# Transposes of the second read on VectorE, and a decode of the weights in three VectorE operations, in a fused attention and MLP kernel

## The chip, the cores and the metric

One Trainium2 chip, one of its cores. The metric is the device time of one execution in microseconds (us). The kernel before took a median of 690.48 us over three runs (689.43 to 690.51).

## The reference

```python
# x [8, 8, 512, 64], state [8, 8, 32, 64] (float32); B, H, S or Ns, D
a     = softmax(scale * x @ state^T, over the 32 states);  xread = a @ state
a2    = softmax(scale * state @ x^T, over the 512 tokens); sread = a2 @ x
attn  = concatenate([xread, sread], axis=2)        # [8, 8, 544, 64]
rows  = attn.transpose(0, 2, 1, 3).reshape(8 * 544, 512)
out   = (maximum(rows @ w_in, 0) ** 2) @ w_out     # w_in [512, 2048], w_out [2048, 512]
```

The weights come as 64-bit floats, so each is two 32-bit words, a low and a high one.

## The kernel before

The work is cut into blocks. Blocks 0 to 7 are the 512 token rows of one batch each; block 8 is the 256 rows of all `sread`. In a block, the hidden layer is cut into 16 chunks of 128 columns (`fc`). For each chunk, `hidden` multiplies on TensorE into a tile `ph` (L688 or, through the helper `mm3`, L306), ScalarE and VectorE make relu and square of it (L697 to L715), and `accumulate` multiplies the result with 128 rows of `w_out` into four accumulators `acc` (L306 or L722). TensorE's order is the next chunk's `hidden`, then this chunk's `accumulate`.

For blocks 0 to 7 the attention is folded into the weights: `make_w2` multiplies the batch's state with `w_in` (tile `w2ps`), 256 or 512 columns at a time, and `hidden` multiplies that `w2` with the softmax `k` of the batch, so `xread` itself is never made. Most operands are split into a high and a low part, and three matmuls (high by high, high by low, low by high) stand for one; that is `mm3`. In block 0, the first eight chunks of `hidden` (`plain_w2`, L688) and the first six of `accumulate` (`plain_wo`, L722) use the f32 values unsplit. `prep_wo` decodes a chunk of `w_out`, `split_wo` splits it.

The attention of a batch runs one block ahead of its use. For a batch from 2 on: `load_p` and `load_n` load x in two layouts, `xp` (in runs of 128 bytes) and `xn`; `prep` transposes `xp` on VectorE into `xT`; `scores` (tile `sc`) multiplies the states with it; `transposed_scores` and `softmax` make `k` on VectorE and ScalarE; `exp_s` (L500) makes the exponentials `e` of the second softmax; `transposes` (L566) turns `e` on TensorE into a tile `pt`, which is copied to `eT`; `sread` (L587) multiplies `eT` with `xn` into `pr`, whose scaled and transposed result goes to the SBUF tile `srall`. `move_sread` collects `srall` for block 8. Batch 0 has a way of its own: `prep` transposes on TensorE (tile `px`), `token_scores` gives `tsc`, and `token_softmax` ends in transposes into `pk` and a copy to `kf`. The tiles `sc`, `w2ps`, `pt`, `pr` and `tsc` share one pair of PSUM banks (`banks`); the tiles `ph` take turns in two others.

`decode` makes an f32 from the two words of a 64-bit float: ScalarE takes the absolute value of the high word (L321); VectorE clamps it (L323), shifts it by three bits and masks (L325), puts sign and top bit in (L327), and the low word's top three bits (L330). `decode_wi` does so for `w_in` (16 tiles `wi_raw`), `prep_wo` for `w_out` (16 tiles `wo_raw`). The result is kept in f32.

The order of everything is written by hand in the strings `FIRST` (blocks 0 to 2 and what goes with them), `BLOCK` (one later block, filled in for blocks 3 to 6), `LAST` and `READS`. A word names a step; a word with a tilde runs the step to its next `yield`, one without runs it to its end. `keep_order` ties each engine's instructions to that order, so every engine's queue, and SyncE's queue of transfers, is in the order of the words. The string `SECOND` lists the steps that take the second of two ways.

Of the kernel before, what the change touches and what calls it, by code (L numbers as in the profile page):

```python
# [14 lines left out]
ALU = mybir.AluOpType
# [25 lines left out]
    token_softmax.0.1 load_wo.5 prep_wo.0 ~hidden.0.0 ~prep_wo.1 ~prep_wo.1 ~prep_wo.1 ~w2.0.1
    hidden.0.0 prep_wo.1 ~hidden.0.1 ~decode_wi.4 ~decode_wi.5 w2.0.1 ~decode_wi.4 ~decode_wi.5 load_wo.6
    ~decode_wi.4 scores.0
    hidden.0.1 ~decode_wi.5 decode_wi.4 accumulate.0.0 ~exp_s.0.0 decode_wi.5 ~exp_s.0.0 ~prep_wo.2 exp_s.0.0
    ~exp_s.0.1 load_wo.7 ~decode_wi.6 ~prep_wo.2 ~exp_s.0.1 ~hidden.0.2 ~prep_wo.2 ~split_wo.0 exp_s.0.1 prep_wo.2
    ~decode_wi.7 ~transposes.0 split_wo.0
    hidden.0.2 ~decode_wi.6 accumulate.0.1 ~decode_wi.7 transposes.0 ~decode_wi.6 ~decode_wi.7 ~decode_wi.6
    ~prep_wo.3 ~decode_wi.7 ~prep_wo.3 ~prep_wo.3 ~prep_wo.3 ~w2.0.2 ~split_wo.1 prep_wo.3 ~hidden.0.3 w2.0.2
    decode_wi.6 decode_wi.7 ~sread.0 split_wo.1
    hidden.0.3 prep_states.1 accumulate.0.2 load_states.2 ~sread.0 ~prep_wo.4 sread.0 start.2 ~prep_wo.4 ~prep_wo.4  # L50
    ~prep_wo.4 ~prep_wo.6 prep_wo.4 ~prep.1.0 ~split_wo.2 ~prep_wo.6 ~prep_wo.6 ~hidden.0.4 split_wo.2 prep.1.0
    ~prep_wo.6 ~prep_wo.5 prep.1.1 prep_wo.6 ~prep.1.2
# [874 lines left out]
```

## Time and profile before

| | |
|---|---|
| median of the runs | 690.48 us |
| the profiled execution | 689.09 us |
| its span, first to last instruction | 687.3 us |
| busy: TensorE, its weight loads, VectorE, ScalarE | 96%, 72%, 53%, 50% |
| busy from 0 to 30 us: TensorE, VectorE, ScalarE | 17.0, 19.1, 13.3 us |
| first `hidden` starts | 27.58 us |
| moved by DMA | 48.47 MB, 79,845 packets |

The profile is one execution on the chip. Times in its rows are in us unless marked ns; L306 is line 306 of the kernel. PE is TensorE, PEld its weight loads (which overlap the matmuls), DVE VectorE, ACT ScalarE, SP SyncE, which issues most transfers. A row of the timeline gives start, length, engine, line, operation, tiles (written, then read) with their shape, and in brackets how long the engine had been idle and who ended that. The chain of waits follows the work that ended last back from its end. A matmul in f32 shows as two records; a transpose shows as one.

### The profile page before, as it was taken

What the parts mean: (1) busy time and instruction counts of PE and PEld (TensorE: products, weight loads), DVE (VectorE), ACT (ScalarE), POOL (GpSimd) and SP (SyncE); (2) the same over time, 40 slices, a digit from 0 to 9 for tenths busy, and PEclk for the clock granted to TensorE, in tenths of its full rate; (3) what the DMA queues carried; (4) which work ended last, traced back from release to release, by engine and by line L of the source; (5) the groups of instructions that cost most, each with busy time, mean ns of one, the idle gap of its engine ahead of it and who ended that gap; (6) DMA issues with size and microseconds to landing.
All of it is one profiled execution on the core that took longest, in us unless ns stands there. A gap on an engine that the chain in (4) does not pass through costs nothing.

```text
span 687.3 us, 9880 instructions
## 1 busy us (share of the span) xinstructions
PE 660.9 (96%) x3904; PEld 497.7 (72%) x3904; DVE 365.7 (53%) x668; ACT 340.8 (50%) x627; POOL 1.2 (0%) x7
## 2 busy tenths in 40 slices
PE   4799999999999999999999999999999999999994
PEld 3444667777777777678777777777767877778993
DVE  4888976889343634554446434552455332235541
ACT  4466656767555544454436434453445444444441
POOL 0000000000000000000000000000000000000000
PEclk9999999999999999999999999999999999999998
DMA  9904351738030553302040024002100011001001
GB/s 319 320 13 112 110 166 33 256 111 185 0 123 1 143 103 80 55 1 55 22 108 1 1 62 116 7 1 62 62 0 1 1 45 48 0 1 50 13 1 31
DMA packets 79845, 48.47 MB, mean 71 GB/s; under 512 B 57912, under 2 KB 66616, under 8 KB 79800
## 3 DMA queue, kind: packets, MB, share of 16 engines
q1 hardware_dynamic: 79256, 47.33, 24.8%
q8 instruction: 30, 0.49, 0.3%
q10 hardware_dynamic: 544, 0.52, 0.3%
q14 instruction: 15, 0.12, 0.1%
HBM read 35.26 MB, written 12.06 MB: 69 GB/s over the span
## 4 chain that ended last, share of the span: by engine, by line
PE 92%; ACT 3%; DVE 2%; DMA 0%; issue 0%; SPq 0%; DVEq 0%; ACTq 0%
PE acc L306 50%; PE ph L306 28%; PE w2ps L311 5%; PE acc L722 3%; PE ph L688 2%; PE pr L587 1%; PE sc L311 1%; PE pt L566 1%; ACT e L500 1%; PE tsc L446 1%; ACT ph L707 0%; ACT ph L708 0%; ACT g_hi L713 0%; DMA std<-in_state_dram 0%; DVE dec L327 0%
## 5 line engine op out<-in xcount | busy, mean ns | idle before, releaser
L306 PE MATMUL acc<-wo,g_hi 128*128 128x512 f32 x1040 | 322.7, 391 | 0.4 <-DVE o L739 0.4
L306 PEld LDWEIGHTS acc<-wo,g_hi 128*128 128x128 f32 x1040 | 193.1, 188 | 43.2 <-issue 2.5
L306 PE MATMUL acc<-wo,g_lo 128*128 128x512 f32 x520 | 202.5, 389 | 0.0
L715 DVE TENSOR_TENSOR g_lo<-ph,g_hi 128x512 fp32r<-128x512 f32 (+1 forms) x138 | 91.0, 659 | 195.3 <-ACT g_hi L713 191.9
L306 PE MATMUL ph<-k_hi,w 128*128 128x512 f32 x480 | 171.8, 399 | 0.0
L707 ACT ACTIVATE ph<-ph 128x512 f32<-128x512 f32 x92 | 53.6, 582 | 158.1 <-PE ph L306 158.1
L306 PEld LDWEIGHTS ph<-k_hi,w 128*128 128x128 f32 x480 | 90.0, 188 | 45.4 <-issue 27.7
L306 PEld LDWEIGHTS acc<-wo,g_lo 128*128 128x128 f32 x520 | 97.6, 188 | 21.1 <-DVE g_lo L715 0.2
L713 ACT CAST g_hi<-ph 128x512 fp32r<-128x512 f32 (+1 forms) x138 | 77.6, 563 | 34.7 <-DVE ph L712 31.8
L306 PE MATMUL ph<-k_lo,w 128*128 128x512 f32 x240 | 93.4, 389 | 0.0
L712 DVE SCALAR_TENSOR_TENSOR ph<-ph,r 128x512 f32<-128x512 f32 (+1 forms) x46 | 27.9, 606 | 63.1 <-ACT r L711 63.1
L711 ACT ACTIVATE r<-ph 128x512 f32<-128x512 f32 (+1 forms) x46 | 24.1, 525 | 71.8 <-PE ph L306 71.8
L708 ACT ACTIVATE ph<-ph 128x512 f32<-128x512 f32 x92 | 53.5, 582 | 2.9
L306 PEld LDWEIGHTS ph<-k_lo,w 128*128 128x128 f32 x240 | 45.1, 188 | 8.2
L645 DVE TENSOR_TENSOR w<-w2ps,w 128x512 fp32r<-128x512 f32 x60 | 38.6, 686 | 18.9 <-ACT w L642 18.9
L642 ACT CAST w<-w2ps 128x512 fp32r<-128x512 f32 x60 | 32.4, 595 | 13.9 <-PE w2ps L311 13.9
L311 PE MATMUL w2ps<-wi,stT 64*32 64x512 f32 (+1 forms) x544 | 35.8, 583 | 2.1 <-ACT e L500 2.1
L306 PE MATMUL ph<-sr_k_hi,s 128*128 128x256 f32 x128 | 25.5, 282 | 0.0
L722 PE MATMUL acc<-deco,gf 128*128 128x512 f32 x48 | 21.9, 599 | 0.0
L306 PEld LDWEIGHTS ph<-sr_k_hi,s 128*128 128x128 f32 x128 | 21.0, 191 | 0.7
L306 PE MATMUL ph<-sr_k_lo,s 128*128 128x256 f32 x64 | 18.1, 283 | 0.0
L311 PEld LDWEIGHTS w2ps<-wi,stT 64*32 64x32 f32 x544 | 6.2, 105 | 16.2 <-issue 10.4
(87 smaller groups left out, 460.2 us busy)
## 6 DMA issues: line engine op xcount, KB each, us to landing
out_dram<-o SPq DMA_DIRECT2D x34, 256.0 KB, 2.5
wi_raw<-in_moe_w_in_dram SPq DMA_DIRECT2D x16, 512.0 KB, 5.2
wo_raw<-in_moe_w_out_dram SPq DMA_DIRECT2D x16, 512.0 KB, 6.7
xp<-in_x_dram SPq DMA_DIRECT2D x96, 64.0 KB, 2.3
part_d<-po SPq DMA_DIRECT2D x8, 256.0 KB, 2.3
o<-part_d SPq DMA_DIRECT2D x8, 256.0 KB, 3.4
xn<-in_x_dram SPq DMA_DIRECT2D x6, 256.0 KB, 8.4
kl<-k_d SPq DMA_DIRECT2D x2, 512.0 KB, 4.0
```

What stands on the lines that cost most here:

```text
L306: T.matmul(ps, l, r, start=first and i == 0, stop=last and i == len(seq) - 1)
L311: T.matmul(ps, l, r, start=True, stop=True)
L642: A.copy(w[:, u, g, 0], ps[g])
L645: V.tensor_sub(w[:, u, g, 1], ps[g], w[:, u, g, 0].bitcast(F32))
L688: T.matmul(ph, w[c][:, cs], k[:, c], start=c == 0, stop=c == G - 1)
L707: A.activation(ph, ph, AF.Relu)
L708: A.activation(ph, ph, AF.Square)
L711: A.activation(r, ph, AF.Relu)
L712: V.scalar_tensor_tensor(ph, ph, 0.0, r, ALU.max, ALU.mult)
L713: A.copy(ghi, ph)
L715: V.tensor_sub(glo, ph, ghi.bitcast(F32))
L722: T.matmul(acc[i], ghi[:, ts(i, P)], wo[fc], start=first, stop=last)
```

## The change

- **Decode.** For all 32 tiles, ScalarE scales the absolute high word by 2 to the 16th, and a second ScalarE operation makes the three low bits from the top byte of the low word, into a new tile `bits` with one buffer. VectorE then clamps, shifts by three and ors the bits, and ors the sign: three operations in place of four.
- **Second read.** For batches 3 to 7 (`b >= ND`), `transposes` runs on VectorE in blocks of 32 by 32 into `eB`; four transfers write it to a tensor in DRAM, `e_d`, and one loads it back as `eT`. `pr` then takes a buffer of `ph` in place of the pair of banks.
- **Read results.** `sread` writes its result to a tensor in DRAM, `sr_d`, and `move_sread` loads it with four transfers in place of sixteen. The columns are ordered by state, then batch, and the last store follows.
- **Dummies.** `keep_busy` issues matmuls of the identity with itself ahead of the first steps of batch 0, into the tile that the step then writes; their number is in `BUSY`, 39 in all.
- **Table.** The first step runs an exponential of one column on ScalarE.
- **Chunk 6** of block 0's `accumulate` is unsplit (`plain_wo`).
- **Order.** At the start, x of batch 0 is loaded ahead of the weights, and the first token scores go ahead of most decodes. From then on `w2` stands later, and `transposes` earlier, than before.

TensorE at the start: `px` transposes of x, `tsc` token scores, `w2ps` the first w2 (before, then changed).

```order
L417 MATMUL px0_0_133<-ident_70,xn0_89 128x128 x4
L417 MATMUL px0_1_140<-ident_70,xn0_89 128x128 x4
L417 MATMUL px0_2_151<-ident_70,xn0_89 128x128 x4
L446 MATMUL tsc0_161<-bd_83,xT0_132 128x64 x8
L417 MATMUL px0_3_177<-ident_70,xn0_89 128x128 x4
L446 MATMUL tsc0_161<-bd_83,xT0_132 128x64 x8
L311 MATMUL w2ps0_0_1_217<-wi0_73,stT_72 32x256
```

In the changed kernel, on the same engine and at the same place:

```order
L319 MATMUL px0_1_141<-ident_70 128x128 x3
L446 MATMUL px0_1_141<-ident_70,xn0_94 128x128 x4
L319 MATMUL px0_2_154<-ident_70 128x128 x2
L446 MATMUL px0_2_154<-ident_70,xn0_94 128x128 x4
L319 MATMUL tsc0_166<-ident_70 128x128 x3
L476 MATMUL tsc0_166<-bd_88,xT0_129 128x64 x8
L319 MATMUL px0_3_188<-ident_70 128x128 x2
L446 MATMUL px0_3_188<-ident_70,xn0_94 128x128 x4
L319 MATMUL tsc0_166<-ident_70 128x128 x4
L476 MATMUL tsc0_166<-bd_88,xT0_129 128x64 x8
L319 MATMUL w2ps0_0_0_235<-ident_70 128x128 x8
L324 MATMUL w2ps0_0_1_236<-wi0_72,stT_71 32x256
```

The steps keep their order; dummies (L319) stand ahead of each, six more ahead of the first `px`.

VectorE at the start, from the last decode operations ahead of the first token softmax (`m10` its maximum, `sp0_0` the subtraction) on, before:

```order
L323 TENSOR_SCALAR dec3_159<-dec3_159 128x512
L325 TENSOR_SCALAR dec3_159<-dec3_159 128x512
L327 SCALAR_TENSOR_TENSOR dec3_159<-wi_raw3_109,dec3_159 128x512
L454 TENSOR_REDUCE m10_0_184<-tsc0_161 128x16
L458 TENSOR_TENSOR sp0_0_192<-tsc0_161,m10_0_184 128x512
L330 SCALAR_TENSOR_TENSOR wi0_73<-wi_raw2_105,dec2_149 128x2x256
```

In the changed kernel, from VectorE's first instruction on:

```order
L383 STREAM_TRANSPOSE stA0_111<-std0_89 128x256
L338 TENSOR_SCALAR dec0_152<-dec0_152 128x512
L340 SCALAR_TENSOR_TENSOR dec0_152<-dec0_152,bits0_164 128x512
L343 SCALAR_TENSOR_TENSOR wi0_72<-wi_raw0_107,dec0_152 128x2x256
L484 TENSOR_REDUCE m10_0_195<-tsc0_166 128x16
L488 TENSOR_TENSOR sp0_0_201<-tsc0_166,m10_0_195 128x512
L338 TENSOR_SCALAR dec1_181<-dec1_181 128x512
L340 SCALAR_TENSOR_TENSOR dec1_181<-dec1_181,bits1_186 128x512
```

Ahead of the first maximum stood fourteen decode operations, of four tiles; now stand three, of one tile.

TensorE in block 3, around chunk 11's hidden (`ph3_11`), with the second read of batch 4, before:

```order
L306 MATMUL acc3_0_3_2464<-wo9_1324,g_hi3_9_2775 128x512 x2
L306 MATMUL acc3_0_3_2464<-wo9_1324,g_lo3_9_2776 128x512
L566 MATMUL pt4_2829<-ident_70,e24_0_2600 128x128 x4
L566 MATMUL pt4_2829<-ident_70,e24_1_2603 128x128 x4
L306 MATMUL ph3_11_2838<-k_hi3_2236,w2_3_4_2630 128x512
```

In the changed kernel:

```order
L314 MATMUL acc3_0_3_2538<-wo9_1339,g_hi3_9_2844 128x512 x2
L314 MATMUL acc3_0_3_2538<-wo9_1339,g_lo3_9_2845 128x512
L324 MATMUL w2ps3_6_2899<-wi3_75,stT_71 32x512 x8
L635 MATMUL pr4_2908<-xn4_2489,eT4_2819 32x64 x32
L314 MATMUL ph3_11_2941<-k_hi3_2321,w2_3_4_2755 128x512
```

The eight transposes are gone; w2 of columns 1536 on and `pr` now stand here, `pr` one chunk sooner than before. SyncE's queue in the same block, changed kernel:

```order
L601 DMA e_d4_84<-eB4_2687 64x16x32 x4
L372 DMA std5_2717<-in_state_dram 32x12x32 x4
L424 DMA xp5_2722<-in_x_dram 32x16x32 x12
L604 DMA eT4_2819<-e_d4_84 128x4x256
L424 DMA xp5_2722<-in_x_dram 32x16x32 x4
L643 DMA sr_d_82<-srt4_2960 512x1x32
L408 DMA xn5_3102<-in_x_dram 128x32x64
```

Before, this queue had the four state loads, all sixteen `xp` loads and `xn` one behind the other; the way of e out and back now frames the state loads and twelve of the `xp` loads.

```diff
 def decode(raw, shape, nm, out=None, tag="dec"):
     low, high = raw[..., 0], raw[..., 1]
     v = p2.tile([P, *shape], U32, tag=tag, name=f"dec{nm}", bufs=DB)
     vf = v.bitcast(F32)
+    if f"bits.{nm}" in second:
+        A.activation(vf, high.bitcast(F32), AF.Abs, scale=2.0**16)
+        yield
+        b = p2.tile([P, *shape], U32, tag="bits", name=f"bits{nm}", bufs=1)
+        A.activation(b, raw.bitcast(U8)[..., 3], AF.Copy, scale=1 / 32, bias=-15.5 / 32)
+        yield
+        V.tensor_scalar(vf, vf, F64_HI_MAX * 2.0**16, F64_HI_MIN * 2.0**16, ALU.min, ALU.max)
+        yield
+        V.scalar_tensor_tensor(v, v, 3, b, ALU.logical_shift_left, ALU.bitwise_or)
+        yield
+        out = v if out is None else out
+        V.scalar_tensor_tensor(out, high, 0x80000000, v, ALU.bitwise_and, ALU.bitwise_or)
+        return out.bitcast(F32)
...
+def keep_busy(key, ps):
+    for _ in range(BUSY.get(key, 0)):
+        T.matmul(ps, ident, ident, start=True, stop=True)
...
+BUSY = {"prep.0": 6, "prep.1": 3, "prep.2": 2, "prep.3": 2, "token_scores.0": 3, "token_scores.1": 4, "w2": 8, "token_softmax.0": 4, "token_softmax.1": 4, "hidden.0.0": 3}
...
 def transposes(self):
     b = self.b
+    if b >= ND:
+        t = p2.tile([P, G, J, 32], F32, tag="wraw", name=f"eB{b}", bufs=RB)
+        for g in range(G):
+            V.transpose(t[:, g].rearrange("p t n -> p (t n)"), self.e2.pop(g).rearrange("p k q -> p (k q)"))
+            yield
+        to = e_d[b].rearrange("(t s) g (j n) -> j s g t n", s=32, n=32)
+        for j in range(NC):
+            SP.dma_start(to[j], t[32 * j : 32 * j + 32])
+        yield
+        eT = p2.tile([P, KC, G, P], F32, tag="wraw", name=f"eT{b}", bufs=RB)
+        SP.dma_start(eT, e_d[b].rearrange("(k p) g q -> p k g q", p=P))
+        self.eT = {g: eT[:, :, g] for g in range(G)}
+        return
...
 def sread(self):
-    t = banks(f"pr{b}")
-    pr = t[:, 0, : G * D].rearrange("p (g d) -> p g d", g=G)
+    if b < ND:
+        pr = banks(f"pr{b}")[:, 0, : G * D].rearrange("p (g d) -> p g d", g=G)
+    else:
+        pr = ps_h.tile([P, G, D], F32, tag="ph", name=f"pr{b}")
...
-    V.transpose(srall[:, :, b * Ns : b * Ns + Ns], srd.rearrange("p g (e d) -> p (g e) d", e=E))
+    srt = p2.tile([P, NC, Ns], F32, tag="srt", name=f"srt{b}", bufs=1)
+    V.transpose(srt, srd.rearrange("p g (e d) -> p (g e) d", e=E))
+    SP.dma_start(sr_d[:, :, b * Ns : b * Ns + Ns], srt)
...
 def first():
+    one = cp.tile([P, 1], F32, tag="one", name="one")
+    PL.memset(one, 1.0)
+    A.activation(one, one, AF.Exp)
...
-    plain_wo: 0.0 0.1 0.2 0.3 0.4 0.5
+    plain_wo: 0.0 0.1 0.2 0.3 0.4 0.5 0.6
...
-    hidden.{b}.8 ~softmax.{n}.0 ~softmax.{n}.1 accumulate.{b}.7 ~w2.{b}.6 ~hidden.{b}.9 ~hidden.{b}.9 ~w2.{b}.6
+    hidden.{b}.10 softmax.{n}.0 softmax.{n}.1 accumulate.{b}.9 ~w2.{b}.6 ~sread.{n} ~hidden.{b}.11 ~w2.{b}.6
```

More of the change, by code (lines that the diff above doesn't have):

```diff
@@ L41 @@
[L41 to L52, printed above, removed]
@@ new lines @@
+    ~split_wo.5 ~softmax.1.1 ~softmax.1.0 ~softmax.1.1 ~softmax.1.0 ~w2.1.0 load_raw.9 ~softmax.1.1 accumulate.0.6
+    ~w2.1.0 split_wo.4 load_wo.8 softmax.1.0 ~softmax.1.1 w2.1.0 ~hidden.0.7 softmax.1.1 split_wo.5 ~hidden.1.0
+    ~split_wo.6
+    hidden.0.7 prep_states.2 ~accumulate.0.7 ~hidden.1.0 exp_s.1.1 split_wo.6 prep.2.0 prep.2.1
+    hidden.1.0 ~hidden.1.1 accumulate.0.7 prep.2.2 prep.2.3 ~transposes.1 start.3 accumulate.1.0 ~hidden.1.1
+    ~decode_wi.8
+    hidden.1.1 ~decode_wi.8 ~hidden.1.2 transposes.1 ~decode_wi.8 ~decode_wi.8 ~hidden.1.2 decode_wi.8 ~sread.1
@@ new lines @@
+    accumulate.1.1 load_n.2.0 ~sread.1
+    hidden.1.2 ~decode_wi.9 sread.1 ~decode_wi.9 ~prep_wo.8 ~decode_wi.9 ~w2.1.2 ~decode_wi.9 decode_wi.9 ~prep_wo.8
+    ~hidden.1.3 ~w2.1.2 ~prep_wo.8 ~prep_wo.8 ~hidden.1.3 w2.1.2 prep_wo.8 scores.2
+    hidden.1.3 ~split_wo.8 accumulate.1.2 transposed_scores.2.0 ~exp_s.2.0 transposed_scores.2.1 ~exp_s.2.0
+    ~softmax.2.0 exp_s.2.0 ~hidden.1.4 ~exp_s.2.1 ~softmax.2.0 ~exp_s.2.1 accumulate.1.3 load_raw.10 ~softmax.2.1
+    ~hidden.1.4 exp_s.2.1 ~softmax.2.1 split_wo.8 ~softmax.2.0
@@ L119 @@
-    ~softmax.3.1 ~softmax.3.1 accumulate.0.10 ~hidden.0.11 w2.0.6 softmax.3.0 ~softmax.3.1
-    hidden.0.11 softmax.3.1 ~hidden.0.12 sread.3 accumulate.0.11 ~hidden.0.12
+    hidden.1.12 ~hidden.1.13 scores.3 ~hidden.1.13 accumulate.1.12 transposed_scores.3.0
+    hidden.1.13 ~exp_s.3.0 transposed_scores.3.1 ~exp_s.3.0 ~hidden.1.14 exp_s.3.0 ~exp_s.3.1 ~hidden.1.14
+    accumulate.1.13 ~exp_s.3.1
+    hidden.1.14 exp_s.3.1 ~w2.0.4 ~transposes.3 ~transposes.3 ~hidden.1.15 ~w2.0.4 ~transposes.3 w2.0.4
@@ new lines @@
+    accumulate.1.14 ~hidden.1.15
+    hidden.1.15 ~hidden.0.8 ~accumulate.1.15 ~hidden.0.8 transposes.3
+    hidden.0.8 ~hidden.0.9 accumulate.1.15 accumulate.0.8 ~hidden.0.9
+    hidden.0.9 ~hidden.0.10 ~softmax.3.0 ~softmax.3.0 accumulate.0.9 ~hidden.0.10 load_part.0 ~softmax.3.1
+    ~softmax.3.1 ~softmax.3.0
+    hidden.0.10 ~softmax.3.1 ~softmax.3.0 ~w2.0.6 ~softmax.3.1 ~softmax.3.0 ~sread.3 ~w2.0.6 ~softmax.3.0
+    ~softmax.3.1 ~hidden.0.11 ~softmax.3.0 ~sread.3 w2.0.6 ~softmax.3.0 accumulate.0.10 ~hidden.0.11 ~softmax.3.1
@@ L121 @@
+    ~softmax.3.1
+    hidden.0.11 ~softmax.3.1 softmax.3.0 ~hidden.0.12 softmax.3.1 sread.3 accumulate.0.11 ~hidden.0.12
     hidden.0.12 ~hidden.0.13 accumulate.0.12 ~hidden.0.13
@@ L145 @@
[L145 to L147 removed]
+    transposed_scores.{n}.1
+    hidden.{b}.4 ~exp_s.{n}.0 ~exp_s.{n}.1 accumulate.{b}.3 ~hidden.{b}.5 ~exp_s.{n}.0 ~exp_s.{n}.1 ~hidden.{b}.5
+    hidden.{b}.5 exp_s.{n}.0 exp_s.{n}.1 ~transposes.{n} ~transposes.{n} ~softmax.{n}.0 ~softmax.{n}.1
@@ new lines @@
+    accumulate.{b}.4 ~hidden.{b}.6 ~transposes.{n} load_states.{m} start.{m} load_p.{m}.0 load_p.{m}.1 load_p.{m}.2
+    ~hidden.{b}.6
+    hidden.{b}.6 ~softmax.{n}.0 ~softmax.{n}.1 accumulate.{b}.5 ~w2.{b}.4 ~hidden.{b}.7 ~w2.{b}.4 ~hidden.{b}.7
+    w2.{b}.4 ~softmax.{n}.0 ~softmax.{n}.1
+    hidden.{b}.7 ~softmax.{n}.0 ~softmax.{n}.1 accumulate.{b}.6 ~hidden.{b}.8 ~hidden.{b}.8
+    hidden.{b}.8 ~softmax.{n}.0 ~softmax.{n}.1 ~softmax.{n}.0 ~softmax.{n}.1 transposes.{n} accumulate.{b}.7
+    ~hidden.{b}.9 load_p.{m}.3 ~hidden.{b}.9 ~softmax.{n}.0 ~softmax.{n}.1
```

198 lines of the change are left out of this document (95 added, 103 removed).

## The prediction

> **What bounds the kernel now.** I read the page's first two parts, then who waited for whom on TensorE from 28 us on, then the chain of waits through the first 70 us, then the operations that the change touches.
>
> ```profile
> PE 660.9 (96%) x3904; PEld 497.7 (72%) x3904; DVE 365.7 (53%) x668; ACT 340.8 (50%) x627; POOL 1.2 (0%) x7
> ...
> PE   4799999999999999999999999999999999999994
> ...
> PE w2ps L311 <- ACT e L500: 2.1, 4, 0.5
> PE sc L311 <- DVE w L645: 1.1, 1, 1.1
> PE ph L688 <- ACT kf L299: 0.7, 1, 0.7
> PE acc L306 <- DVE o L739: 0.4, 1, 0.4
> ```
>
> TensorE is busy for 96% of the span. The digits show where it is not: the first two slices of 17 us, and the last, where the output drains. The four lower rows are all its waits from 28 us on, 4.3 us. So behind the start only fewer matmuls or fewer of these waits shorten the kernel; a lighter VectorE (53%) does not by itself. The start is another matter:
>
> ```profile
> 5.70 1.28 ACT L299
> ...
> 8.46 0.67 ACT dec L321
> ...
> 9.15 0.44 DVE dec L323
> ...
> 15.86 0.69 DVE dec L327
> ...
> 17.18 0.70 DVE sp L458
> ...
> 18.02 3.66 PE tsc L446 x16
> ...
> 26.94 0.60 ACT kf L299
> ...
> 27.58 3.51 PE ph L688 x4
> ...
> 31.68 1.91 PE ph L688 x4
> ```
>
> Columns are start, length, work. One after the other: the activation table (1.28 us), the decode of four `wi` tiles, which keeps VectorE from 9.15 to 16.55, the first token softmax, the second token scores, the copy of the last part of `kf`, and at 27.58 the first hidden matmul, the point from which TensorE is full. That hidden takes 3.51 us, the next one, of the same work, 1.91.
>
> ```profile
> 10.07 2.27 PE L417 MATMUL px<-ident,xn 128*128 128x128 f32 x8 [4.65 <-DMA xn<-in_x_dram]
> 12.14 3.52 PE L446 MATMUL tsc<-bd,xT 128*128 128x64 f32 x16
> ...
> 51.45 0.87 PE px L417 x8
> ...
> 28.00:31.00 3.00, 3.00 (x4) 0.76 (x3) 2.90 (x8) 0.00 (x0) 0.00 (x0) 1.00 0.96 341
> ```
>
> Eight transposes take 2.27 us at 10 us and 0.87 at 51 us. So TensorE runs at about half rate until some 31 us, though the granted clock (1.00, the third column from the end of the last row) does not show it. It did not speed up in 5.6 us of transposes and token scores (10.07 to 15.66), and did behind 3.5 us of 512-column matmuls. By these ratios eight token scores take about 1.8 us at full rate, an estimate.
>
> **The start, new order.** The table load (1.28) now runs while the data come, three of the four `wi` decodes go behind the first token softmax, and x is loaded ahead of the weights. What is late next is the data:
>
> ```profile
> 9.29 0.67 ACT L321 ACTIVATE dec<-wi_raw 128x512 f32<-128x512 f32 x1 [0.17 <-DMA wi_raw<-in_moe_w_in_dram]
> 16.80 0.57 ACT L299 COPY xT<-px 128x512 f32<-128x512 f32 x1
> 22.81 0.65 ACT L299 COPY w<-w2ps 128x256 f32<-128x256 f32 x2 [3.14 <-PE w2ps L311]
> 23.34 0.65 ACT L460 ACTIVATE sp<-sp 128x512 f32<-128x512 f32 x1
> ...
> 24.04 0.68 DVE L463 TENSOR_REDUCE s<-sp 128x16 f32<-128x512 f32 x1
> 25.25 0.76 DVE L470 TENSOR_TENSOR pp<-sp,s 128x256 f32<-128x256 f32 x2
> ```
>
> The first row waited for the second weight tile: states, half of x and two tiles, 1.63 MB, queued up to its end. In the new order the first tile ends at that same place, so it lands at 9.29; all of x ends 0.5 MB sooner, 1.5 us at 341 GB/s, so at 7.8. ScalarE is in order: behind its wait for that tile stand the scaling (0.67) and the second `xT` copy (0.57), so the first token scores cannot start before 10.55, whatever TensorE does.
>
> With TensorE at full rate by then: scores to 12.35; VectorE, held by one decode until 12.5 (0.44 and two steps of 0.69), max and subtraction (0.7 each) to 13.9; second scores to 15.9; VectorE's queue to 17.8; eight dummies and w2 to 18.3; copies and exponential (0.65 each) to 19.6; sum to product 1.97 (24.04 to 26.01) to 21.5; four transposes (0.11 each) and copy (0.60) to 22.7; hidden to 24.6, against 31.09: 6.5 us. Then w2 of the next 256 columns waits for two decodes of 1.8 us each behind 21.5, until 25.2, which gives 0.65 back: 5.9. If full rate comes only as the first token scores start, the transposes and dummies before them take 6.7 us from 7.0 on, so these start at 13.7, and hidden ends at 27.1: 4.0. I take **-4.7**, between them, since the rows show no speeding up from short matmuls alone.
>
> A dummy is a 128x128 matmul in f32, two records. 512 columns at half rate cost 0.85 us a record (four in 3.51), so 128 columns 0.21, a dummy 0.43, and half of that at full rate. All 39 are 8.4 us at full rate, which lie in TensorE's waits; 17 at half rate, which do not all fit (a rival, below).
>
> **Where TensorE is full.** Pieces of a later block, an unsplit accumulate, and all transposes of e:
>
> ```profile
> 276.44 1.36 PE ph L306 x6
> 277.80 2.72 PE acc L306 x12
> ...
> 304.07 1.02 PE w2ps L311 x16
> ...
> 313.49 0.87 PE pt L566 x8
> ...
> 54.91 3.44 PE acc L722 x8
> ...
> L566 PE MATMUL pt<-ident,e 128*128 128x128 f32 x64 | 8.3, 272 | 0.0
> ```
>
> - The transposes of e for batches 3 to 7 leave TensorE: 5 x 0.87 = **-4.35** (by busy time 40 of 64 in 8.3, or 5.2, for the range). VectorE's two each are far from the path at 53%.
> - In blocks 3 to 6, w2 of columns 1024 on goes one hidden and one accumulate later, past the exponentials that hold its pair of banks: the four waits go, **-2.1**. Late next is w2's own split, some 2.5 us of copies and subtractions, under 2.72 + 1.36 of matmuls.
> - `sc` waited 1.1 behind w2 of batch 1. VectorE's decodes there are shorter, but more of them are queued: between 0 and -1.1, I take **-0.5**.
> - Chunk 6 of block 0 goes unsplit: 3.44 in place of 2.72: **+0.7**.
> - VectorE between batch 1's scores and `hidden.1.0`:
>
> ```profile
> 61.99 0.72 DVE L488 STREAM_TRANSPOSE sp<-sc 128x512 f32<-128x512 f32 x1 [0.72 <-PE sc L311]
> ...
> 74.88 1.28 DVE L645 TENSOR_TENSOR w<-w2ps,w 128x512 fp32r<-128x512 f32 x2
> ...
> 76.20 0.39 PE L306 MATMUL ph<-k_hi,w 128*128 128x512 f32 x1
> ```
>
> It has no gap from 61.99 to 76.16, and the hidden that needs its result starts at 76.20. Now three operations of chunk 6 (1.8) join and one g_lo (0.6) leaves, 15.3 us against 15.0 of matmuls: **+0.4**, from 0 to 1.2.
> - The decode itself:
>
> ```profile
> L321 ACT ACTIVATE dec<-wi_raw 128x512 f32<-128x512 f32 x16 | 10.6, 671 | 3.4 <-DMA wi_raw<-in_moe_w_in_dram 3.4
> ...
> L325 DVE TENSOR_SCALAR dec<-dec 128x512 uint32<-128x512 uint32 x16 | 6.5, 424 | 0.3
> ...
> 31.00:41.00 10.00, 10.00 (x74) 4.75 (x74) 8.13 (x21) 7.07 (x15) 0.00 (x0) 1.00 0.22 55
> ```
>
> VectorE loses 32 x 0.42; ScalarE gains 32 operations that read one byte of eight. None such is in the trace; nearest is L321, four bytes of eight, 0.67. I take that, from 0.57 (a plain copy) to 1.3 (twice). In block 0 ScalarE then is at 71% plus 11 x 0.67 over 43 us, some 88%. An accumulate comes 4 to 5 us of matmuls after its hidden; relu and square need 1.3, so four operations queued ahead are hidden. So I cost it at nothing; without that cover it is the third rival. `bits` has one buffer, so ScalarE also waits for VectorE's second step of the decode before; following both queues I find under 1 us each time, inside that cover.
> - The outputs drain as before, with the same bytes in rows of the same length.
>
> Sum: -4.7 - 4.35 - 2.1 - 0.5 + 0.7 + 0.4 = -10.55. The profiled execution took 689.09 us (span 687.3 and 1.8 around it), 1.4 below the median of 690.48; taken off the median, the sum gives **679.9**.
>
> **Rivals.** *Half rate lasts.* For it: 10.07 to 15.66. If only a stretch like the 3.5 us at 27.58 ends it, the first is the eight dummies ahead of w2 (8 x 0.43 = 3.4). Then the dummies push: scores from 13.7, the second ones done at 24.4, w2 at 28.4, hidden at 34.5, 3.4 late. Sum -2.45: 688.0. Chance 0.13. The Trainium skill, "TensorE: Matmul & The Clock Gate", Part 1, has about 3.4 us of sustained activity before the array's clock doubles, in windows that run freely, and its Part 4 says that transposes do not count as activity. By that rule this rival or the next is what happens; the trace agrees with it (5.6 us without effect, 3.5 us with).
>
> *Half rate until the second token scores.* First scores to 17.2, hidden to 29.1, 2.0 gained: 682.6. Chance 0.2.
>
> *ScalarE full in block 0.* With `bits` at 1.3 us it has 30 + 14 us of work in 43; TensorE waits 1.7 at the least, some 3 since the work comes in lumps: 682.9. Chance 0.08.
>
> *Slower: e comes back late.* For blocks 3 to 6, e goes to DRAM in pieces of 128 bytes and back, and on SyncE's queue four state loads (0.48 each) and twelve `xp` loads stand between the two ways.
>
> ```profile
> 346.55 8.31 SPq L397 DMA_DIRECT2D xp<-in_x_dram x16
> ...
> DMA to landing us min/median/max: 3.3/4.0/4.7
> ...
> DMA to landing us min/median/max: 1.8/2.3/3.7
> ```
>
> An `xp` issue takes 0.52; `kl`, of eT's size, lands in 4.0 (second row), `xp`, in pieces of 128 bytes, in 2.3 (third). So 2.0 + 1.9 + 6.2 + 0.4 + 4.0 = 14.5 us, under five accumulates, four hiddens and two w2: 5 x 2.72 + 4 x 1.36 + 2 x 1.02 = 21. The writes have 8 us before they hold up eT. If they take 15 more than that, each block waits 8.5, in all some 38: 718. It turns the sign from 2.7 us beyond the cover in each block. For it: no write of such pieces is in the trace. Against: `xp`. Chance 0.04. The Trainium skill, "DMA: Bandwidth & Descriptors", Specifications, says that below 512 bytes a DMA engine reads, modifies and writes. By that rule the writes take longer than `xp`; no row shows it.
>
> **How the numbers follow.** The forecast has 0.55, the rivals as given. Low end: full rate from the first transposes (-5.9), 5.2 for the transposes, -1.1 for `sc`, nothing lost ahead of `hidden.1.0`: -13.6, and 1.05 by which the lowest run (689.43) lay below the median: 675.8. High end: the second rival with ScalarE's 3 us, 685.6. Outside lie the first rival and the slower one, 0.17. A measurement can tell about 0.2%, 1.4 us, from no change. Every case but the slower one is 2.4 us or more below; with accidents that I did not see: faster 0.93, same 0.03, slower 0.04.
>
> **What would show it.** Right: the first hidden ends at 24 to 27.5 us and takes about 1.8; no `pt` from batch 3 on; no wait of w2 for an exponential; chunk 6's accumulate in 3.4. Wrong: `px` and `tsc` still at 0.27 and 0.22 a record beyond 20 us, `pr` waiting for a DMA, or relus of block 0 held behind `bits`.

## The result, and the profile after

The changed kernel takes 670.69 us, the median of four runs (670.59 to 670.80), against 690.29 (689.43 to 690.51) for the kernel before on the same chip: a ratio of 0.9718, 95% interval 0.9702 to 0.9735. It is 19.6 us faster, where 10.6 were forecast, and 670.7 lies below the range of 675.8 to 685.6. Its profiled execution took 670.59 with a span of 668.7, so by spans 18.6 us went; the rest is that the profiled run of before (689.09) lay 1.2 below its median.

From the page of the changed kernel, engines and the digits of TensorE:

```profile
PE 659.5 (99%) x3938; PEld 499.6 (75%) x3938; DVE 358.1 (54%) x645; ACT 357.0 (53%) x654; POOL 1.2 (0%) x8
...
PE   8999999999999999999999999999999999999997
```

TensorE is busy for 99% of the span. The first two slices and the last, which were 4, 7 and 4, are 8, 9 and 7: both ends of the kernel filled up. The start comes first, the chain of waits of the changed kernel (start, length, work):

```profile
8.63 0.67 ACT dec L333
...
13.18 1.16 PE tsc L319 x8
...
22.97 1.98 PE ph L740 x4
24.95 1.19 PE w2ps L324 x16
26.15 1.91 PE ph L740 x4
...
67.86 3.63 PE acc L774 x8
71.49 1.40 PE ph L314 x6
```

The first hidden ends at 24.95 in place of 31.09, 6.1 earlier, and takes 1.98 in place of 3.51. The first weight tile's decode starts at 8.63, and four dummies (eight records, 1.16) stand on the path ahead of the second token scores. The w2 behind it waits for its decode (1.19, where 0.59 is its own time), so 5.5 are left at the second hidden. At 67.86 stands chunk 6's unsplit accumulate, and `hidden.1.0` follows it at 71.49 with no wait. When the rate came is seen on TensorE's own rows of the changed kernel (line 319 are the dummies):

```profile
5.47 1.49 PE L319 MATMUL px<-ident 128*128 128x128 f32 x6
6.75 1.01 PE L446 MATMUL px<-ident,xn 128*128 128x128 f32 x4
...
8.05 0.60 PE L446 MATMUL px<-ident,xn 128*128 128x128 f32 x4
...
9.15 1.90 PE L476 MATMUL tsc<-bd,xT 128*128 128x64 f32 x16
```

Four transposes take 1.01 at 6.75 and 0.60 at 8.05; sixteen token scores take 1.90, against 3.52 before. The rate doubled at about 7.5 us.

Now the blocks. Rows of the chain of before, from one batch's scores to the next's:

```profile
280.52 1.02 PE sc L311 x16
...
354.88 1.02 PE sc L311 x16
...
363.43 1.36 ACT e L500 x4
...
364.83 1.09 PE w2ps L311 x16
```

The same stretch of the changed kernel:

```profile
273.85 1.05 PE sc L324 x16
...
304.97 1.02 PE w2ps L324 x16
305.99 1.03 PE pr L635 x64
...
346.48 1.05 PE sc L324 x16
```

A block, from scores to scores, took 74.36 and takes 72.63, so 1.73 less; the sum had 0.87 + 0.52 = 1.39. No w2 waits for an exponential, and the second read (`pr`) stands directly behind a w2.

The largest piece that the forecast did not have is the end. The last copies of `o` on VectorE, first before, then after:

```profile
677.54 0.69 DVE o L297
```

```profile
664.07 0.69 DVE o L305
```

From there to the end of the span it is 687.3 - 678.23 = 9.07 us before and 668.7 - 664.76 = 3.94 after: 5.1 us. The share of the 16 DMA engines that was busy, in tenths and 40 slices: before in the window from 676 to 688 us, and after from 662 to 669 us.

```profile
DMA  0000000002504012312222222222222100000000
```

```profile
DMA  0000000000000000003997799999820000000000
```

Before, the drain goes at two tenths for most of its time (a mean share of 0.26 from 682 to 684 us), what 4 of 16 engines give; after, at seven to nine tenths. The bytes and the 2 KB rows are the same. What differs is the shape of the two last stores: 4x32x512 before, 16x8x512 after, since block 8's columns are now ordered by state and then by batch.

### The profile page after: what moved, and what is told of

The parts are those of the page before. It is cut to its first block, busy times and chain, and to the rows that moved or that the text cites. A ratio compares the mean times of both kernels' runs of the same rounds, so it can differ in the third digit from the quotient of the medians.

```text
span 668.7 us, 9988 instructions
## 1 busy us (share of the span) xinstructions
PE 659.5 (99%) x3938; PEld 499.6 (75%) x3938; DVE 358.1 (54%) x645; ACT 357.0 (53%) x654; POOL 1.2 (0%) x8
## 4 chain that ended last, share of the span: by engine, by line
PE 97%; DMA 1%; DVE 1%; ACT 1%; issue 0%
PE acc L314 53%; PE ph L314 29%; PE w2ps L324 5%; PE acc L774 4%; PE ph L740 2%; PE sc L324 1%; PE pr L635 1%; DMA wi_raw<-in_moe_w_in_dram 1%; DMA xn<-in_x_dram 0%; PE pt L611 0%; PE w2ps L319 0%; PE px L446 0%; PE tsc L476 0%; PE tsc L319 0%; ACT w L693 0%
## 5 line engine op out<-in xcount | busy, mean ns | idle before, releaser
L314 PE MATMUL acc<-wo,g_hi 128*128 128x512 f32 x1032 | 319.2, 391 | 0.0
L774 PE MATMUL acc<-deco,gf 128*128 128x512 f32 x56 | 25.6, 600 | 0.0
L531 ACT ACTIVATE e<-sc,nb 128x512 f32<-128x512 f32 x16 | 11.0, 687 | 17.0 <-DVE m L525 8.6
L774 PEld LDWEIGHTS acc<-deco,gf 128*128 128x128 f32 x56 | 10.2, 190 | 12.3 <-issue 11.1
```

The lines of the kernel that those rows point to most:

```text
L314: T.matmul(ps, l, r, start=first and i == 0, stop=last and i == len(seq) - 1)
L774: T.matmul(acc[i], ghi[:, ts(i, P)], wo[fc], start=first, stop=last)
```

## The experiments

Ratios are to the kernel before, run in the same group on the same chip (its medians there were 689.7 to 690.5).

**The end: the last stores' shape alone, undone and done.** In the changed kernel (e1) the shape of before comes back:

```
-        by_state = [v.rearrange("p c (n b) -> p c b n", b=B) for v in (hi, lo)]
-        yield from split(*by_state, t.rearrange("p c (b n) -> p c b n", b=B), "sr_lo")
+        yield from split(hi, lo, t, "sr_lo")
...
-                n = P // B
-                rows = out_v[:, S + n * i : S + n * i + n].rearrange("b n f -> n b f")
-                pick(f"store.{i}", SP, A).dma_start(rows, o)
+                pick(f"store.{i}", SP, A).dma_start(out_v[4 * i : 4 * i + 4, S : S + Ns], o)
```

> The changed kernel with block 8's columns batch-major again, so that its two last stores are 4x32x512 (as in the kernel before) in place of 16x8x512; nothing else differs. Theory (the last store is spread over as many DMA engines as its outer dimension allows, 4 before and 16 after): the end comes back, 9.1 us from the last copy to the span's end in place of 3.9, so +5.1 on 670.7, about 675.8 us, with a DMA share near 0.25 behind the last copy. Rival (the shorter end has another cause, such as which queue the stores are issued on or what else is still in flight): no change, 670.7.

In the kernel before (e2) the same edit is made the other way round.

> The kernel before with only block 8's columns ordered by state and the two last stores as 16x8x512. Theory of the engines: -5.1 on 690.3, about 685.2 us, the end 3.9 us long. Rival (the end is short for another part of the change): 690.3. If the strided split (2.2 us in place of 1.05 on ScalarE) held up TensorE, it would be above 685.2; I expect it off the path.

Measured: e1 677.22 us, 0.9819 (0.9793 to 0.9844); e2 685.48, 0.9927 (0.9913 to 0.9942). From the last copy to the span's end e1 needs 9.0 us (669.77 to 678.8) and e2 3.97 (679.73 to 683.7). e2 gained 5.0, as expected. e1 lost 6.5 by medians rather than 5.1. Its profiled run is its slowest (680.68), and there the surplus is in the start, taken up below: the second hidden starts at 31.07 us in place of 26.08. The surplus of the faster runs has no trace. The drain of e1, from 670 to 679 us, goes at two tenths again:

```profile
DMA  0252062022222222222222222222212100000000
```

**A third shape.** Each store of the changed kernel is cut into two of 8x8x512:

```
-                pick(f"store.{i}", SP, A).dma_start(rows, o)
+                for h in range(2):
+                    pick(f"store.{i}", SP, A).dma_start(rows[8 * h : 8 * h + 8], o[64 * h : 64 * h + 64])
```

> The changed kernel with each of block 8's stores cut into two of 8x8x512, on the same queue. Theory (engines by the outer dimension): each half runs on 8 engines. From 9.07 us with 4 engines and 3.94 with 16, an end of a + c/k has a 2.2 and c 27.4, so with the same 8 for all halves 5.65 us, a DMA share of about 0.5, +1.7, 672.4 us. If the second halves go to the other 8 engines: 3.9 and 670.7. Rival (what counts is the size of a transfer or the order of rows, not the outer dimension): 3.9, 670.7, with the share at 0.8 or more.

Measured: 673.57 us, 0.9775 (0.9742 to 0.9809); the end is 5.8 us long (666.10 to 671.9). Its drain, from 664 to 672 us:

```profile
DMA  0000000000000345354555125545543100000000
```

Mostly four to five tenths, so an outer dimension of 4, 8 and 16 gives shares of about two, five and seven to nine tenths, and ends of 9.07, 5.8 and 3.94 us. Four issues were queued here in place of two, some 0.6 us each; how much of the 5.8 is theirs was not measured. The other 1.3 us by which this run's span is longer are in its start (second hidden at 27.43). The Trainium skill, "DMA: Bandwidth & Descriptors", section "Why a DMA increments its semaphore by 16 and not by 1", says that a DMA uses the largest number of engines up to 16 that divides the slowest dimension of both its sides; the three shapes agree.

**A batch's transposes, the late w2 and the second read, each by itself.** e6 is the changed kernel with the transposes of e on TensorE for batches 3 to 7 (`ND = B`, and their words in the order back behind an accumulate):

```
-    ND = 3
+    ND = B
...
-            if b < ND:
+            if b < 3:
                 pr = banks(f"pr{b}")[:, 0, : G * D].rearrange("p (g d) -> p g d", g=G)
```

> The changed kernel with the transposes of e for batches 3 to 7 on TensorE again, two per block behind an accumulate as in the kernel before; the second read's own place and its PSUM bank stay as changed. Prediction's term: 5 x 0.87 = 4.35, so 675.0 us. By busy time of eight matmul records, 5.2, so 675.9. Rival (the return trip of e through DRAM costs something that this gives back): under +4.

e7 is the kernel before with w2 of columns 1024 on moved:

```
-    hidden.{b}.5 ~softmax.{n}.1 exp_s.{n}.0 exp_s.{n}.1 ~softmax.{n}.0 accumulate.{b}.4 ~w2.{b}.4 ~hidden.{b}.6
-    load_states.{m} start.{m} load_p.{m}.0 load_p.{m}.1 load_p.{m}.2 load_p.{m}.3 ~hidden.{b}.6 ~w2.{b}.4
+    hidden.{b}.5 ~softmax.{n}.1 exp_s.{n}.0 exp_s.{n}.1 ~softmax.{n}.0 accumulate.{b}.4 ~hidden.{b}.6
+    load_states.{m} start.{m} load_p.{m}.0 load_p.{m}.1 load_p.{m}.2 load_p.{m}.3 ~hidden.{b}.6
...
-    hidden.{b}.6 w2.{b}.4 ~softmax.{n}.1 ~softmax.{n}.1 accumulate.{b}.5 ~hidden.{b}.7 ~hidden.{b}.7 ~softmax.{n}.0
+    hidden.{b}.6 ~softmax.{n}.1 ~softmax.{n}.1 accumulate.{b}.5 ~w2.{b}.4 ~hidden.{b}.7 ~w2.{b}.4 ~hidden.{b}.7 w2.{b}.4 ~softmax.{n}.0
```

> The kernel before with only one step moved: in blocks 3 to 6 w2 of columns 1024 on goes behind the next accumulate, past the next batch's exponentials. Prediction's term: four waits of 0.52, -2.1, so 688.2 us against 690.3. By the length of a block (the w2 behind the wait also takes 1.09 in place of 1.02): 4 x 0.6 = -2.4, 687.9. Rival (the split of the later w2 is late and a hidden waits for it): 690 or more.

e8 is the changed kernel with the second read of batches 4 to 7 one accumulate further on:

```
-    hidden.{b}.10 softmax.{n}.0 softmax.{n}.1 accumulate.{b}.9 ~w2.{b}.6 ~sread.{n} ~hidden.{b}.11 ~w2.{b}.6
-    ~sread.{n} ~hidden.{b}.11 w2.{b}.6 sread.{n}
-    hidden.{b}.11 accumulate.{b}.10 ~hidden.{b}.12 ~hidden.{b}.12
+    hidden.{b}.10 softmax.{n}.0 softmax.{n}.1 accumulate.{b}.9 ~w2.{b}.6 ~hidden.{b}.11 ~w2.{b}.6
+    ~hidden.{b}.11 w2.{b}.6
+    hidden.{b}.11 accumulate.{b}.10 ~sread.{n} ~hidden.{b}.12 ~sread.{n} ~hidden.{b}.12 sread.{n}
```

> The changed kernel with the second read of blocks 3 to 7 taken from right behind a w2 to behind the next accumulate, so that two groups of small matmuls no longer stand next to each other. Theory (each change between the 512-column stream and a group of small matmuls costs some 0.22 us beyond the group's own time, as the 1.58 in place of 1.36 of the hidden behind a w2 shows): a block from scores to scores takes 0.2 us longer, 72.85 in place of 72.63, and the time rises by 0.9 to 1.0, to 671.7. Rival (the place does not matter): 72.63 and no change.

Measured: e6 674.91 us, 0.9790 (0.9747 to 0.9833); e7 687.78, 0.9965 (0.9951 to 0.9978); e8 672.73, 0.9760 (0.9730 to 0.9790). The unedited changed kernel, run beside e6 and e8 as a control (below), took 671.13 and 673.03, so by medians e8 shows no loss. The medians carry the unsteady start of the changed kernel, so I read the block from scores to scores. The chain of e6:

```profile
274.50 1.05 PE sc L324 x16
297.48 0.87 PE pt L611 x8
...
348.05 1.05 PE sc L324 x16
```

The chain of e7:

```profile
281.97 1.02 PE sc L311 x16
...
355.70 1.02 PE sc L311 x16
```

And of e8:

```profile
273.92 1.05 PE sc L324 x16
...
310.40 1.03 PE pr L635 x64
311.43 1.58 PE ph L314 x6
...
346.81 1.05 PE sc L324 x16
```

Transposes back: 73.55 in place of 72.63, 0.92 a block. Late w2: 73.73 in place of 74.36, 0.63. Second read apart: 72.89, 0.26; the row behind `pr` shows where: the hidden takes 1.58 in place of 1.36 behind each group of small matmuls, and with `pr` next to a w2 there is one such place fewer. Together 1.81 for the 1.73 that a block lost. In the three kernels the steps stand alone, and their sum is the block's gain within 0.1. Over the whole stretch from batch 3's scores to the last copy of `o`, e6 takes 4.4 more than its control, e7 2.4 less than the kernel before and e8 1.0 more than the changed kernel.

**The dummies and the decode.** e3 has `BUSY = {}`, e4 has the line `bits: ...` taken out of the table (so all 32 decodes are as before), e5 has only the dummies up to the first token scores:

```
-BUSY = {"prep.0": 6, "prep.1": 3, "prep.2": 2, "prep.3": 2, "token_scores.0": 3, "token_scores.1": 4, "w2": 8, "token_softmax.0": 4, "token_softmax.1": 4, "hidden.0.0": 3}
+BUSY = {"prep.0": 6, "prep.1": 3, "prep.2": 2, "prep.3": 2, "token_scores.0": 3}
```

> The changed kernel without any of the 39 dummy matmuls. Theory (the six dummies ahead of the first transposes bring TensorE to full rate at about 7 us): without them transposes and token scores go at half rate, 0.22 us a record of 64 columns in place of 0.11, the first hidden ends 3 to 4 us later than 24.95, time about 674 us. Rival 1 (the new order is what matters, the dummies only cost): 1.2 us of dummies ahead of the second token scores and 1.8 ahead of w2 leave the path, so about 668.5 us. Rival 2 (half rate until a long stretch, as the forecast's first rival has it): over 676 us.

> The changed kernel with the decode of before (one ScalarE operation and four on VectorE) for all 32 tiles; order of the source and all else as in the changed kernel. Theory (the decode is worth little, since VectorE has slack except in the start and in block 0): three decodes of the start are 0.42 us longer each on VectorE, so +0.4 to +1.5, 671.1 to 672.2 us. Rival 1 (VectorE bounds block 0, where it would get 10 more us of work into 43 us at 85%): +3 or more, 674 us. Rival 2 (ScalarE's 0.68 us a tile is on the path): faster, 670 us or less.

> The changed kernel with the 16 dummies up to the first token scores only; the 23 behind them (second token scores, w2, transposes of the products, first hidden) are gone. Theory A (once at full rate TensorE stays there through waits of 1 to 2 us): 1.2 us of dummies ahead of the second scores and 1.8 ahead of w2 leave the path, hidden starts at 20 to 21.5 us in place of 22.97, time 668 to 669.5 us. Theory B (the rate falls back when TensorE waits): the first hidden takes 3.5 us again and the short matmuls before it twice as long, time 672 to 674 us, as without dummies (672.9).

Measured: e3 672.90 us, 0.9746 (0.9731 to 0.9760); e4 673.25, 0.9758 (0.9739 to 0.9777); e5 672.10, 0.9731 (0.9704 to 0.9759). TensorE's rows without dummies:

```profile
6.65 2.23 PE L446 MATMUL px<-ident,xn 128*128 128x128 f32 x8 [0.38 <-DMA xn<-in_x_dram]
8.90 3.65 PE L476 MATMUL tsc<-bd,xT 128*128 128x64 f32 x16
...
23.88 3.48 PE L740 MATMUL ph<-kf,w 128*128 128x512 f32 x4 [0.68 <-ACT kf L307]
```

All at half rate up to 27.4 us. So the dummies do bring the rate, but they are the smaller part of the start's 5.5: 2.2 us by medians, and 1.7 by the second hidden of the profiled runs (27.88 against 26.15). Without them the first hidden ends at 27.36, still 3.7 ahead of the kernel before. That larger part belongs to the new order, the earlier table load and the new decode together; the table load (ScalarE's 5.70 to 6.98 before, at 1.21 now) was not run by itself. With the early dummies alone TensorE falls back when it waits, as theory B had it, though by medians e5 is not clear of the control beside it (671.13):

```profile
19.67 0.68 PE L510 MATMUL pk<-ident,pp 128*128 128x128 f32 x4 [1.61 <-DVE pp L500]
21.56 1.08 PE L510 MATMUL pk<-ident,pp 128*128 128x128 f32 x4 [1.21 <-DVE pp L500]
23.32 3.78 PE L740 MATMUL ph<-kf,w 128*128 128x512 f32 x4 [0.68 <-ACT kf L307]
```

What the old decode costs is not clear. By medians it is 2.6 us, but this group had no control, and e4's ratio is that of the slowest control below (0.9757). In its profiled run the second hidden starts 1.1 later (27.21 against 26.15). Its weights wait for the second of two decodes:

```profile
26.58 0.64 PE L323 MATMUL w2ps<-wi,stT 64*32 64x256 f32 x8 [0.38 <-DVE wi L356]
```

The other 0.7 stand already at the second token scores (13.87 against 13.18), and there two things besides the decode's length were late: the first weight tile, whose decode starts at 9.06 in place of 8.63, and the full rate, which came at about 9.5 us, so that the first scores ran until 12.2. So of e4's loss only some 0.4 us is shown to be the decode's. Rival 1 does not hold in the profiled run: from 30 to 72 us VectorE is busy for 39.3 of 42, and TensorE for all 42. The two slower runs (673.96 and 674.92) have no trace.

**The unsteady start.** The changed kernel itself, with no edit, ran three times more as a control:

> The changed kernel itself, unchanged, as a control beside the kernels of its group. Its first runs gave 670.6 to 670.8 us. In the no-dummies run and its fellows the start varied by 1 to 5 us from run to run (the first weight tile landed between 8.6 and 10.1 us, in one run the granted clock was 0.50 from 11 to 22 us). If that is the start of this kernel in general, the control shows a spread of 1 us or more; if it was those kernels alone, 670.7.

> The changed kernel unchanged, a control for its group: 670.4 to 671.8 us as before.

> The changed kernel unchanged: 670.4 to 671 us in most runs, and 674 to 677 in any in which the first weight tile lands beyond about 10 us.

Measured: 671.13 us (670.41 to 671.83), 0.9718; 673.03 (670.38 to 676.38), 0.9757; 671.86 (671.27 to 674.22), 0.9742. In the second of them two runs took 670.4 and 670.6 with a mean granted clock of 0.998 and more, and two took 675.5 and 676.4 with 0.992 and 0.991. TensorE's rows of the profiled one, 676.4:

```profile
11.46 1.10 PE L476 MATMUL tsc<-bd,xT 128*128 128x64 f32 x8 [1.84 <-ACT xT L307]
...
14.81 2.08 PE L319 MATMUL tsc<-ident 128*128 128x128 f32 x8 [1.30 <-DVE sp L488]
16.68 3.52 PE L476 MATMUL tsc<-bd,xT 128*128 128x64 f32 x16
```

The first weight tile landed at 10.26 (8.61 in the run above). ScalarE decodes it ahead of the second copy of `xT`, so the first token scores waited 1.84 us for that copy; then the rate fell, and the granted clock of the same run shows it (third value from the end):

```profile
18.00:20.00 2.00, 2.00 (x12) 2.00 (x11) 0.00 (x0) 0.00 (x0) 0.00 (x0) 0.50 1.06 393
```

To show that the wait is the cause, e12 loads the first two weight tiles in the other order, so that the tile is late on purpose, and e13 has, beside that, twelve dummies in place of three in front of the wait (`"token_scores.0": 12`):

```
-    load_states.0 start.0 load_n.0.0 first load_n.0.1 load_n.0.2 load_n.0.3 load_raw.0 load_raw.1 ~prep_states.0
+    load_states.0 start.0 load_n.0.0 first load_n.0.1 load_n.0.2 load_n.0.3 load_raw.1 load_raw.0 ~prep_states.0
```

> The changed kernel with its first two weight tiles loaded in the other order, so that the tile which the first decode needs lands as the second, 1.5 us later, at about 10.2 us in place of 8.6. Theory (ScalarE waits for it ahead of the second copy of xT, so TensorE has nothing for some 2 us behind the first transposes; the rate falls to half, as in the control's two slow runs where the tile landed at 10.3): granted clock 0.5 from about 12 us on, first hidden ends at 29 to 31, time 675 to 677 us in most runs. Rival (the fall comes at random, not from the wait): +1.5 only, 672 us, and the odd run higher.

> The late-tile kernel with 12 dummies in place of 3 ahead of the first token scores, 0.23 us each, so that TensorE's wait for the late tile is filled. Theory (it is TensorE's idling that lets the rate fall): no fall, first hidden ends near 26.5, 672 to 673 us, below the late-tile kernel by 3 or more. Rival (the late data itself, or something outside the kernel, does it): 675 or more, like the late-tile kernel.

Measured: e12 674.98 us (673.26 to 677.14), 0.9788 (0.9765 to 0.9811), with a mean clock of 0.991 to 0.994 in three of its four runs; e13 672.85 (672.00 to 673.56), 0.9755 (0.9741 to 0.9770), with 0.999 to 1.0 in all four. TensorE's rows of e12, then of e13:

```profile
12.41 1.97 PE L476 MATMUL tsc<-bd,xT 128*128 128x64 f32 x8 [2.59 <-ACT xT L307]
```

```profile
8.02 2.84 PE L319 MATMUL tsc<-ident 128*128 128x128 f32 x24
...
12.46 1.10 PE L476 MATMUL tsc<-bd,xT 128*128 128x64 f32 x8 [0.75 <-ACT xT L307]
...
16.80 1.90 PE L476 MATMUL tsc<-bd,xT 128*128 128x64 f32 x16
```

With the tile just as late (its decode starts at 11.22 and 11.27) the filled kernel keeps the full rate. So it is TensorE's idling, not the late data, that lets the rate fall. It need not fall: the expected difference was 3 or more, and the medians differ by 2.1 and the intervals of the ratios just touch, since e12 was back at full rate at 19 us, the control only at 23.6, and one run of e12 (mean clock 0.999) hardly fell.

**Can the start be better?** e10 moves dummies off the path (the four of the second token scores to the last transposes of x, the eight of w2 behind it, `"prep.3": 6` and `"token_softmax.0": 12`); e11 takes ScalarE's copies of `xT` and the first softmax steps ahead of the first decode; e14 is both, with `"prep.3": 5` and `"token_softmax.0": 6`. The edit of e11 to the table of the first blocks:

```
-    prep.0.0 load_wo.2 ~decode_wi.0 ~prep.0.2 prep.0.1 load_raw.6 ~decode_wi.0 token_scores.0.0 prep.0.2
-    ~decode_wi.0 ~decode_wi.0 ~decode_wi.1 load_raw.7 decode_wi.0 ~decode_wi.1 ~prep.0.3 ~token_softmax.0.0
-    ~decode_wi.2 load_wo.7 ~token_softmax.0.0 prep.0.3 ~token_softmax.0.0 ~decode_wi.1 token_scores.0.1 load_wo.3
+    prep.0.0 load_wo.2 ~prep.0.2 prep.0.1 load_raw.6 token_scores.0.0 prep.0.2 ~prep.0.3 ~decode_wi.0
+    ~token_softmax.0.0 load_raw.7 ~decode_wi.0 ~token_softmax.0.0 prep.0.3 ~token_softmax.0.0 ~decode_wi.0
+    ~decode_wi.0 ~decode_wi.1 decode_wi.0 ~decode_wi.1 ~decode_wi.2 load_wo.7 token_scores.0.1 ~decode_wi.1 load_wo.3
```

> The changed kernel with the same number of dummies, but those that stood on the path moved to where TensorE waits anyway: the four ahead of the second token scores go ahead of the last transposes of x, the eight ahead of w2 go behind it, ahead of the first transposes of the products. Theory (dummies must fill the waits, not lengthen the path): second scores end some 0.7 earlier, w2 another 0.8 earlier, TensorE stays at full rate, the first hidden starts at 21.3 to 22 in place of 22.9, time 669 to 670 us. Rival (a wait that is now bare lets the rate fall): first hidden 3.5 us long, time 672 or more.

> The changed kernel with ScalarE's copies of x and VectorE's first two steps of the token softmax ahead of the first decode, so that nothing up to the second token scores waits for a weight tile; the dummies are as changed. Theory (the first scores no longer wait for the tile): first scores done at about 10.5 in place of 11.0, the first softmax step no longer behind the decode, first hidden ends 0.5 to 1.5 earlier than 24.95, 669.3 to 670.2 us, and no run with a fallen clock. Rival (the decode of two tiles then ends last and holds w2): 671 or more.

> The x-first kernel with the dummies of the path moved into waits: none ahead of the second token scores and of w2, five ahead of the last transposes of x, six and four ahead of the transposes of the products. Theory (both together): another 0.7 to 1.5 us less than the x-first kernel, 668 to 669.5 us. Rival (a bare wait lets the rate fall): 672 or more.

Measured: e10 669.75 us (668.78 to 670.08), 0.9705 (0.9690 to 0.9719); e11 669.85 (669.60 to 670.02), 0.9712 (0.9696 to 0.9729); e14 669.87 (669.60 to 669.96), 0.9712 (0.9697 to 0.9726). TensorE's row of e11:

```profile
22.22 1.98 PE L740 MATMUL ph<-kf,w 128*128 128x512 f32 x4
```

In e11 the tile's decode starts at 9.49, later than in the changed kernel, and the hidden still starts 0.75 earlier. Every run of the three lies below every one of the 16 runs of the changed kernel (670.38 at the least), but the gain is under 1 us, only e10 ran on the chip of one of the controls (the second), and the intervals of the ratios overlap. Together they gain nothing more: in e10 the moved dummies hold up the products' transposes until 20.3, and in e14 w2 waits for the second decode:

```profile
16.48 0.64 PE L324 MATMUL w2ps<-wi,stT 64*32 64x256 f32 x8 [1.75 <-DVE wi L343]
```

e15 is e11 with batch 2's transposes off TensorE too (`ND = 2`), its second read next to the w2 of block 2's columns 512 on.

> The x-first kernel with batch 2's transposes of e on VectorE and through DRAM as well, and its second read next to the w2 of block 2's columns 512 on. Theory (a batch's transposes cost TensorE 0.87, and the second read next to a w2 saves 0.2 to 0.3 more): 1.1 below the x-first kernel's 669.8, 668.7 us, 2 us below the control. Rival 1 (three more steps of VectorE and a second tile of the weights' ring around batch 2 make a weight decode late): 670 or more, with a wait of w2 or of an accumulate between 110 and 150 us. Rival 2 (the x-first order gains nothing on an equal chip): about 669.6.

Measured: 673.79 us (671.02 to 673.96), 0.9764 (0.9750 to 0.9777), against 0.9742 for the control of the same group: a miss. The profiled run is its fastest (671.02); the other four took 673.67 to 673.96, and no trace shows what they lost. The chain of the profiled run, from 118 us on:

```profile
127.56 5.41 DMA wi_raw<-in_moe_w_in_dram
...
133.05 0.66 ACT dec L333
...
136.03 3.29 PE acc L314 x12
```

As the chain reads, it is rival 1: the additional tile of e stays in the weights' ring until the second read, a weight tile is loaded late, and ScalarE's decode, which waits for it, stands in front of a relu for which an accumulate waits. Whether another place for the second read avoids that was not tried. Its w2 at 85.01 was 1.5 ahead of the control's (86.53); at 143.40 it is 0.4 ahead (143.79).

## Why the prediction was wrong

The direction and the mechanisms of the larger terms were right; the time missed the range because of a step that was costed at nothing. By spans the sum of -10.55 came out as -18.6: 5.5 in the start, 0.7 back for chunk 6, 8.65 from batch 3's scores to the last copy of `o`, and 5.1 in the end.

- **The step that failed: "The outputs drain as before, with the same bytes in rows of the same length."** It cost 0 in the sum and was worth -5.1, as e1, e2 and e9 show. The store was looked at for its bytes and rows; how many engines it runs on was not. The rows were there: before's digits, two tenths for most of the drain, say that a quarter of the engines moved the last bytes. Without this the kernel would have come to about 675.8, just the low end of the range: the other terms were too small as well, by some 3 us in all.
- **The start, -4.7: measured -5.5.** It lay between the two bounds given (-5.9 and -4.0). The one that had full rate by the first scores is right, and the w2 that waits for its decode gave back 0.6 of the 6.1, as worked out (0.65). That a value between the two came so near is in part luck: it leaned towards the case "full rate comes only as the first token scores start", which fell, since the rate came at about 7.5 us. That scores could not start before 10.55 was wrong too; eight of the sixteen records need the first copy of `xT` only, and the tile landed at 8.61, not 9.29.
- **The transposes, -4.35: -4.4** (e6). **The w2 behind the exponentials, -2.1: -2.4** (e7); the wait of 0.52 also made the w2 and what follows it longer.
- **Not in the sum at all: the second read next to a w2, 0.26 in each of five blocks, -1.3, and the wait of `acc` for `o` (0.4 in its row), with it some 0.7 around 264 us.** (The 0.26 was measured on four of the five; the 0.7 is what is left of the 1.85 between batch 3's scores and batch 4's, less 0.92 and 0.26.) The first is a change of order that the prediction did not see as one: the 1.58 and 2.94 behind a group of small matmuls stand in the rows of before. The second was quoted, and its fate left open; why it went no run shows. These two and the two terms before make 8.8 by the single runs, against the 8.65 of the two kernels, where 6.45 was forecast.
- **`sc`, -0.5: 0.** It still waits 1.1. **Chunk 6, +0.7: 3.63 in the rows, right. Ahead of `hidden.1.0`, +0.4: 0**, it follows the accumulate at once.
- **The decode at nothing: right beyond the start as far as the profiled runs show.** The byte operation takes 0.68 as bounded, and ScalarE was not full: busy for 31.9 of 42 us (76%) from 30 to 72 us, where some 88% was estimated. In the start at least some 0.4 us hangs on it (e4); the forecast had this inside the -4.7 and not as a term.

Of the rivals none came true in the profiled run. *Half rate lasts* did not: the rate came 3.8 us after TensorE's first matmul (3.69), out of transposes and dummies alone, without a stretch of long matmuls. *Half rate until the second token scores* is close to what the control's runs of 675 and 676 us show, but by a fall from full rate, not by a late rise; that the rate can fall again in a wait was in none of the rivals. *e comes back late* did not happen: the 128-byte writes landed in 3.2 us (median of 20 issues) and no `pr` waits for a DMA.

## What to carry to other kernels

Read the end of a kernel like any other stage: how many of the 16 DMA engines does the last store use, and does its outer dimension allow 16? When instructions move, count the places where the long matmul stream is broken, not only the time of the short ones. Dummy matmuls can pay where TensorE would wait for a microsecond or more: such a wait let the rate fall in some runs and not in others. Better still is an order in which an engine in line does not wait for a late transfer ahead of work whose data are there.
